# Attention and two MLPs on one core: output stores put off by two steps, a third query buffer, weight stores in tile five, softmax of three batches summed per head by ScalarE

## The chip, the core and the metric

The kernel runs on one core of one Trainium2 chip. TensorE (PE) multiplies, ScalarE (ACT), VectorE (DVE) and GpSimd (POOL) do the elementwise work, and SyncE (SP) issues every DMA of the program, in order, from one queue. Each engine takes its instructions in a fixed order and waits where one is not ready. The metric is the time of one execution on the device in microseconds (us).

## The reference

Three steps follow one another; all data are float32, and the kernel's products keep nearly that precision.

```
# attention, batch 8, heads 8, 576 queries, 64 columns; keys and values are mean-pooled by 8 (72 rows)
scores = q @ k_p.T / sqrt(64); scores -= max(scores); attn = exp(scores)
x = (attn / (sum(attn) + 1e-9)) @ v_p            # -> 4608 tokens x 512
h = x @ w_in1;  x = leaky(h, 0.01) @ w_out1      # 512 -> 2048 -> 512
h = x @ w_in2;  out = relu(h)**2 @ w_out2        # 512 -> 2048 -> 512
```

## The kernel before

**Products.** A float32 product is made of three matmuls (`three`, L271): each operand is split into a high part, cast by ScalarE, and the low rest, subtracted by VectorE. So every operand needs a ScalarE instruction and a VectorE instruction ahead of the matmul.

**First part, up to about 750 us.** The first MLP runs over six tiles of 512 tokens (tile 0 to 5), each as 16 units `f` of 128 hidden columns. `first(t, f)` makes `h` and splits its activation `g` into `gh` and `gl`; `second(t, f)` adds to the four accumulators `acc`. The weights `w` stay decoded in SBUF, and `split_weights` splits them again for each tile into a tile `hl` (a pool of four). In tile 1 those splits are also written to DRAM (`WD`, L190 to L198), from where the later part loads them. Writes that are put off by some ticks pass through `later` and `tick`.

**Work laid between the units.** The generator `attention()` yields after each small step, and the main loop (L900) takes 3 steps per unit in tile 0 and 5 in the later tiles, until the attention is done (in tile 3). A batch has five chunks of 128 or 64 queries: `load_q` fetches a chunk two ahead, `stage_a` transposes it, `stage_b` makes scores `s`, maximum `mx`, exponentials `x`, sums `sm` and the weights `p`, `stage_c` transposes `p`, and `stage_d` makes four output blocks `o` per span, which ScalarE copies to `xo` and SP stores to `x0` in DRAM. `load_x(t + 1)` reads tile t + 1 back from `x0` three units before the tile ends, into `xs`, and `split_x` splits it. `prepare_sums` (`s`, `hs`) and `prepare_products` (`ops`, `hl2`, with its loads `st2`) prepare weight sums for the later part in the same gaps.

**Second part, from about 750 us.** The remaining tokens of the first MLP and then the second MLP run with seven instead of eight block products (`first2`, `second2`), with the weights streamed from `WD`.

**What sets the order.** The program is written in the order above; a list scheduler then orders each engine's instructions by its own estimate, so what stands where on an engine (SP's DMAs too) is read from the built program. In rows of that program `xs1_2_0` is block 0 of the load for tile 2, `xo3_1_0` block 0 of batch 3's second span, `mx1_320_0` the maximum of batch 1's chunk that begins at query 320, `hl_in_4_8` the split of tile 4's unit 8, and the number at a name's end is a counter.

Of the kernel before, what the change touches and what calls it, by code (L numbers as in the profile page):

```python
# [8 lines left out]
F32 = mybir.dt.float32  # L9
# [8 lines left out]
P = 128  # L18
# [9 lines left out]
def raw(ap):  # L28

    return ap.bitcast(F32)  # L30
# [3 lines left out]
def attention_two_mlps(  # L34
# [11 lines left out]
    nc = tc.nc  # L46
    B, H, S, D = q.shape
# [7 lines left out]
    NF = DFF // P  # L55
    RG = KR * H // 2
    SPANS = (320, 256)
    EARLY = 1
    AHEAD = 5
    RATES = (3, 5)  # L60
    HT = 384
    NTILE = 6
# [10 lines left out]
    one_stack = ctx.enter_context(ExitStack())  # L73
    tpool = one_stack.enter_context(tc.tile_pool(name="t", bufs=6))
    hlpool = one_stack.enter_context(tc.tile_pool(name="hl", bufs=4))
    xpool = one_stack.enter_context(tc.tile_pool(name="x", bufs=6))
    gpool = one_stack.enter_context(tc.tile_pool(name="g", bufs=2))
    w_late = one_stack.enter_context(tc.tile_pool(name="w1_late", bufs=NQ))
    w_early_stack = one_stack.enter_context(ExitStack())
# [7 lines left out]
    def temp(name, dt=F32):  # L87
        return tpool.tile([P, TT], dt, tag="t", name=name)

    def work(name, n=TT, early=False):  # L90
        if early:
            return ps_a.tile([P, n], F32, tag="acc", name=name)
        return ps_w.tile([P, n], F32, tag="w", name=name)
# [17 lines left out]
    def place(g):  # L111

        if g < PLAIN:
            return g // TT, g % TT, TT
        return NTILE + (g - PLAIN) // HT, (g - PLAIN) % HT, HT
# [5 lines left out]
    def later(n, **kw):  # L121
        LATE.append([n, kw])

    def tick(n=1):

        for one in LATE:
            one[0] -= n
        while LATE and LATE[0][0] <= 0:
            nc.sync.dma_start(**LATE.pop(0)[1])
# [52 lines left out]
    def split_weights(kind, t, f):  # L182

        w = W[kind, f]
        hl = hlpool.tile([P, 2, TT], F32R, tag="hl", name=f"hl_{kind}_{t}_{f}")
        hi, lo = hl[:, 0], hl[:, 1]
        nc.scalar.copy(hi, w)
        nc.vector.tensor_tensor(out=lo, in0=w, in1=raw(hi), op=ALU.subtract)  # L188
        HL[kind, t, f] = (hi, lo)
        if t == 1:  # L190
            p, i = f % NQ, f // NQ
            for j in range(2):
                part = {(0, 0): 0, (0, 1): 1, (1, 1): 2}.get((i, j) if kind == "in" else (j, i))
                if part is not None:
                    later(
                        2, out=WD[1, kind, p // 2][part, :, p % 2].rearrange("p (h x) -> p h x", h=2),
                        in_=raw(hl)[:, :, j * HD:(j + 1) * HD],
                    )  # L198
# [72 lines left out]
    def three(outp, a, b, first, last, **kw):  # L271

        (ah, al), (bh, bl) = a, b
        nc.tensor.matmul(outp, ah, bh, start=first, stop=False, **kw)  # L274
        nc.tensor.matmul(outp, ah, bl, start=False, stop=False, **kw)  # L275
        nc.tensor.matmul(outp, al, bh, start=False, stop=last, **kw)  # L276


    def attention():

        with ExitStack() as s:
            qp = s.enter_context(tc.tile_pool(name="qp", bufs=2, side="right"))
            ap1 = s.enter_context(tc.tile_pool(name="ap1", bufs=1, side="right"))
            xp = s.enter_context(tc.tile_pool(name="xp", bufs=3, side="right"))
# [151 lines left out]
            for b in range(B):  # L436
                at = 0
                for span in range(len(SPANS)):
                    off = 0
                    while off < SPANS[span]:  # L440
                        n = min(P, SPANS[span] - off)
                        chunks.append((b, span, at, off, n))
                        at, off = at + n, off + n

            qn, qt = {}, {}

            def load_q(b, span, at, off, n):
                qn[b, at] = qp.tile([P, H, D], F32, tag="q", name=f"q{b}_{at}", bufs=2)
                nc.sync.dma_start(out=qn[b, at][:n], in_=q[b, :, at:at + n, :].rearrange("h p d -> p h d"))

            def stage_a(b, span, at, off, n):
# [11 lines left out]
            def stage_b(b, span, at, off, n):  # L463
# [3 lines left out]
                for e in range(2):  # L467
# [10 lines left out]
                    nc.vector.tensor_reduce(out=mx[:n], in_=sc[:n], axis=AX.X, op=ALU.max, negate=True)  # L478
                    if b < EARLY:
                        for h in range(4):  # L480
# [7 lines left out]
                    )  # L488
                if b >= EARLY:
                    nc.scalar.activation(x[:n], x[:n], AF.Exp)  # L490
# [39 lines left out]
            def stage_d(b, span):  # L530
                n = SPANS[span]
                g0 = b * S + sum(SPANS[:span])
                for m in range(NP):
                    o = work(f"o{b}_{span}_{m}")[:, :n]
                    three(
                        o, tuple(t[:, m].rearrange("p a d -> p (a d)") for t in vM),
                        (pt_h[:, m, :n], pt_l[:, m, :n]), True, False,
                    )
                    nc.tensor.matmul(o, vR[:, m], pt_r[:, m // 2, :n], start=False, stop=True)
                    done = 0  # L540
                    if g0 < TT:
                        done = min(n, TT - g0)
                        xh, xl = X[1, 0][m]
                        nc.scalar.copy(xh[:, g0:g0 + done], o[:, :done])
                        nc.vector.tensor_tensor(
                            out=xl[:, g0:g0 + done], in0=o[:, :done], in1=raw(xh[:, g0:g0 + done]), op=ALU.subtract
                        )
                    if done < n:
                        xo = xp.tile([P, SPANS[0]], F32, tag="xo", name=f"xo{b}_{span}_{m}", bufs=2)
                        nc.scalar.copy(xo[:, done:n], o[:, done:n])  # L550
                    while done < n:
                        t, at, wide = place(g0 + done)
                        step = min(n - done, wide - at)
                        nc.sync.dma_start(
                            out=x0[t][m * P:(m + 1) * P, at:at + step], in_=xo[:, done:done + step]
                        )
                        done += step
                    yield

# [10 lines left out]
            for i in range(len(chunks) + 1):  # L570
                if i < len(chunks):
                    b = chunks[i][0]
# [16 lines left out]
                if i > 0:  # L589
                    b, span = chunks[i - 1][:2]  # L590
# [11 lines left out]

    ready = [0]
    att = attention()


    X, XS = {}, {}
# [7 lines left out]
    def load_x(t):  # L615
        XS[t] = []
        for c in range(NK):
            st = temp(f"xs1_{t}_{c}")
            nc.sync.dma_start(out=st, in_=x0[t][c * P:(c + 1) * P, :])
            XS[t].append(st)  # L620

    def split_x(t):
        new_x(t)
        for (hi, lo), st in zip(X[1, t], XS.pop(t)):
            nc.scalar.copy(hi, st)
            nc.vector.tensor_tensor(out=lo, in0=st, in1=raw(hi), op=ALU.subtract)
# [255 lines left out]
        prepare_weights(w1)  # L882
        w1 += 1

    at_work, made, due = True, 0, 0
    prep, preparing, hooks = None, True, 0
    sums1 = prepare_sums()

    def advance():
        nonlocal at_work, made  # L890
        made += 1
        if next(att, 1):
            at_work = False

    split_weights("in", 0, 0)
    split_weights("out", 0, 0)
    first(*units[0])
    split_weights("in", 0, 1)
    x2pool, xg = None, iter(())
    for i, (t, f) in enumerate(units):  # L900
        if f == NF - 3 and t + 1 < NTILE:
            while ready[0] * S < min((t + 2) * TT, NT):
                advance()
            load_x(t + 1)
        if f == NF - 1 and t + 1 < NTILE:
            split_x(t + 1)

        rate = RATES[min(t, 1)]
        if i + 1 < len(units):
            first(*units[i + 1])  # L910
        tick()
        if i + 2 < len(units):
            split_weights("in", *units[i + 2])
        if i + 1 < len(units):
            split_weights("out", *units[i + 1])
        while at_work and made < due + rate // 2:
            advance()
        second(t, f)
        tick()
        due += rate  # L920
        while at_work and made < due:
            advance()
        if w1 < NF:
            prepare_weights(w1)
            w1 += 1
        elif t > 0:
            next(sums1, None)
        if not at_work:
            if prep is None:
                ppool = ctx.enter_context(tc.tile_pool(name="prep", bufs=1, side="right", reuse_waits="tile"))  # L930
                prep = prepare_products()
            for _ in range(3):
                if preparing and next(sums1, 1) and next(prep, 1):
                    preparing = False
        if t == NTILE - 1 and f >= NQ:
            if x2pool is None:
                assert not at_work and next(sums1, 1)
                w_early_stack.close()
                x2pool = ctx.enter_context(tc.tile_pool(name="x2", bufs=1, side="right", reuse_waits="tile"))
                ring = ctx.enter_context(tc.tile_pool(name="ring", bufs=RING, side="right", reuse_waits="tile"))  # L940
                load_x2(0)
                tick(9)
                blocks.insert(0, next_block())
            else:
                if not XO:
                    xg = products_x(0)
                next(xg, None)
# [47 lines left out]
```

## Time and profile before

| | |
|---|---|
| time, median of 3 runs | 1690.49 us (1690.46 to 1691.48) |
| profiled execution: its own time, its span | 1693.28 us, 1691.6 us |
| busy in the span: PE, DVE, ACT, POOL | 1624.4, 1233.9, 840.5, 135.1 us |
| DMA | 403.87 MB, 239 GB/s over the span |

The span goes from the first to the last instruction; 1.7 us of the profiled time lie around it. A busy PE is a PE with a matmul under way, so the difference to the span is time in which it had none. A stage in which PE has no idle time can only be shortened on PE itself.

### The profile page before, as it was taken

The page shows a single profiled execution, that of the slowest core. Times are in us where ns is not written, and L with a number is a line of the kernel's source. Part 1 is how long each engine was busy: PE and PEld are TensorE (multiplying, and loading weights), DVE is VectorE, ACT ScalarE, POOL GpSimd, SP SyncE. Part 2 cuts the span into 40 slices and gives each one's busy share as a digit, 9 for nine tenths or more (in the row PEclk, how much of TensorE's full clock was granted, in tenths as well). Part 3 has the DMA queues.
Part 4 walks back from the last instruction along what each step waited for, and adds up shares of the span by engine and source line. Part 5 has one row for each costly group of instructions (what it writes and reads, how often), then busy time and mean ns, then how long its engine had stood idle before and what let it go on. Part 6 is the DMA issues. An engine that isn't in the chain of part 4 may idle for free.

```text
span 1691.6 us, 26132 instructions
## 1 busy us (share of the span) xinstructions
PE 1624.4 (96%) x9688; PEld 1498.5 (89%) x9688; DVE 1233.9 (73%) x1825; ACT 840.5 (50%) x1377; POOL 135.1 (8%) x149
## 2 busy tenths in 40 slices
PE   4888999799999999999999999999999999999998
PEld 3666787677888888889999999999999999999998
DVE  5899988899867988885736648559378477486484
ACT  5666655555656767765535424325334234244233
POOL 3122223222220000000000000000000000000000
PEclk7799999899999999999999999999999999999999
DMA  7644667775623756878888988988988889888886
GB/s 179 185 156 152 190 212 234 229 228 167 201 60 125 255 197 220 292 255 299 292 288 255 303 275 252 310 263 269 307 252 284 287 256 296 277 249 274 265 254 203
DMA packets 215807, 403.87 MB, mean 239 GB/s; under 512 B 55424, under 2 KB 119936, under 8 KB 215680
## 3 DMA queue, kind: packets, MB, share of 16 engines
q1 hardware_dynamic: 215680, 402.19, 74.0%
q8 instruction: 78, 1.28, 0.3%
q14 instruction: 49, 0.40, 0.1%
HBM read 314.57 MB, written 85.98 MB: 237 GB/s over the span
## 4 chain that ended last, share of the span: by engine, by line
PE 74%; DVE 12%; DMA 6%; ACT 3%; issue 2%; SPq 2%; POOL 0%; DVEq 0%; ACTq 0%; POOLq 0%
PE acc L276 12%; PE acc L275 12%; PE h L274 12%; PE h L276 12%; PE acc L274 12%; PE h L275 12%; DMA st_in_out<-in_moe_w_out_dram 2%; DMA wd_out<-hl_out 1%; DVE gl L644 1%; DVE hl_out L188 1%; PE s L470 1%; SPq L332 1%; DVE hl_in L188 1%; DMA rk<-in_k_dram 1%; DVE v L313 1%
## 5 line engine op out<-in xcount | busy, mean ns | idle before, releaser
L690 ACT CAST oh<-g 128x768 fp32r<-128x768 f32 x224 | 187.2, 836 | 284.2 <-PE acc L275 163.6
L274 PE MATMUL h<-xh,wb_in 128*128 128x384 f32 x896 | 299.4, 334 | 1.0 <-ACT s L779 1.0
L275 PE MATMUL h<-xl,wb_in 128*128 128x384 f32 x896 | 299.3, 334 | 0.0
L276 PE MATMUL h<-xh,wb_in 128*128 128x384 f32 x896 | 299.3, 334 | 0.0
L691 DVE TENSOR_TENSOR ol<-g,oh 128x768 fp32r<-128x768 f32 x224 | 213.6, 955 | 102.1 <-ACT oh L690 101.3
L276 PE MATMUL acc<-wb_out,ol 128*128 128x256 f32 x1008 | 282.2, 280 | 0.0
L274 PE MATMUL acc<-wb_out,oh 128*128 128x256 f32 x1008 | 281.2, 279 | 0.0
L275 PE MATMUL acc<-wb_out,oh 128*128 128x256 f32 x1008 | 281.2, 279 | 0.0
L275 PEld LDWEIGHTS acc<-wb_out,oh 128*128 128x128 f32 x1008 | 189.5, 188 | 0.0
L276 PEld LDWEIGHTS acc<-wb_out,ol 128*128 128x128 f32 x1008 | 189.2, 188 | 0.0
L274 PEld LDWEIGHTS acc<-wb_out,oh 128*128 128x128 f32 x1008 | 188.5, 187 | 0.0
L785 DVE TENSOR_TENSOR g<-h,s 128x768 f32<-128x768 f32 x32 | 30.6, 956 | 196.1 <-PE h L276 120.9
L274 PEld LDWEIGHTS h<-xh,wb_in 128*128 128x128 f32 x896 | 168.2, 188 | 1.3 <-ACT s L779 1.3
L275 PEld LDWEIGHTS h<-xl,wb_in 128*128 128x128 f32 x896 | 168.2, 188 | 0.0
L276 PEld LDWEIGHTS h<-xh,wb_in 128*128 128x128 f32 x896 | 168.2, 188 | 0.0
L274 PE MATMUL acc<-gh,hl_out 128*128 128x512 f32 x384 | 150.9, 403 | 8.8 <-ACT gh L643 8.7
L274 PE MATMUL h<-xh,hl_in 128*128 128x512 f32 x384 | 154.2, 402 | 3.3 <-DVE x L486 2.3
L275 PE MATMUL acc<-gl,hl_out 128*128 128x512 f32 x384 | 151.0, 397 | 6.5 <-DVE gl L644 6.4
L276 PE MATMUL h<-xh,hl_in 128*128 128x512 f32 x384 | 151.6, 395 | 2.2 <-DVE hl_in L188 2.2
L275 PE MATMUL h<-xl,hl_in 128*128 128x512 f32 x384 | 150.9, 393 | 0.0
L276 PE MATMUL acc<-gh,hl_out 128*128 128x512 f32 x384 | 149.2, 394 | 0.4 <-DVE hl_out L188 0.3
L694 DVE TENSOR_TENSOR g<-g,g 128x768 f32<-128x768 f32 x128 | 120.8, 955 | 6.7 <-ACT g L752 5.2
(148 smaller groups left out, 2960.6 us busy)
## 6 DMA issues: line engine op xcount, KB each, us to landing
wb_in<-wd_in SPq DMA_DIRECT2D x224, 512.0 KB, 4.3
wb_out<-wd_out SPq DMA_DIRECT2D x224, 512.0 KB, 4.5
xs<-x SPq DMA_DIRECT2D x16, 768.0 KB, 6.7
out_dram<-o SPq DMA_DIRECT2D x24, 384.0 KB, 5.0
k<-in_k_dram SPq DMA_DIRECT2D x64, 128.0 KB, 3.4
q<-in_q_dram SPq DMA_DIRECT2D x32, 256.0 KB, 4.8
st_in_out<-in_moe_w_in_dram SPq DMA_DIRECT2D x16, 512.0 KB
st_in_out<-in_moe_w_out_dram SPq DMA_DIRECT2D x16, 512.0 KB, 4.7
```

The lines of the kernel that those rows point to most:

```text
L188: nc.vector.tensor_tensor(out=lo, in0=w, in1=raw(hi), op=ALU.subtract)
L274: nc.tensor.matmul(outp, ah, bh, start=first, stop=False, **kw)
L275: nc.tensor.matmul(outp, ah, bl, start=False, stop=False, **kw)
L276: nc.tensor.matmul(outp, al, bh, start=False, stop=last, **kw)
L313: nc.vector.tensor_tensor(out=dst if n == D else src[:, :, 0:n], in0=src[:, :, 0:n], in1=src[:, :, n:2 * n], op=ALU.add)
L332: nc.sync.dma_start(out=ts[-1][a * KM:(a + 1) * KM, m % 2], in_=src[b, heads[m][a], 0:KM * POOL, :].rearrange("(kk j) d -> kk (j d)", j=POOL),
L470: nc.tensor.matmul(sc[:n, 2 * m:2 * m + 2].rearrange("p a x -> p (a x)"), qT[:, 2 * e + m, :n], kT[b % 2][:, 2 * e + m].rearrange("p a x - ...
L644: nc.vector.tensor_tensor(out=gl, in0=g, in1=raw(gh), op=ALU.subtract)
L690: nc.scalar.copy(hi, src)
L691: nc.vector.tensor_tensor(out=lo, in0=src, in1=raw(hi), op=ALU.subtract)
L694: nc.vector.tensor_tensor(out=out_, in0=a, in1=b, op=ALU.subtract)
L785: nc.vector.tensor_tensor(out=g11, in0=v, in1=s1, op=ALU.add)
```

## The change

It has five parts. (1) The softmax form that batch 0 alone used (`EARLY`) is used for batches 0 to 2: ScalarE makes the exponentials per head, straight from the scores, with the maximum as bias, and sums them in the same instruction; in the other form VectorE subtracts the maximum and sums. (2) The stores of `xo` go into a list, and are issued when two further attention steps have been made, or just ahead of `load_x`; `xo` has three buffers instead of two. (3) The query tile has three buffers instead of two. (4) The splits of the plain weights are written to DRAM in tile 4 (the fifth) instead of tile 1. (5) The pool of split activations has 5 buffers per tag instead of 6.

```
-    EARLY = 1
+    EARLY = 3
...
-    xpool = one_stack.enter_context(tc.tile_pool(name="x", bufs=6))
+    xpool = one_stack.enter_context(tc.tile_pool(name="x", bufs=5))
...
-        if t == 1:
+        if t == NTILE - 2:
...
-                qn[b, at] = qp.tile([P, H, D], F32, tag="q", name=f"q{b}_{at}", bufs=2)
+                qn[b, at] = qp.tile([P, H, D], F32, tag="q", name=f"q{b}_{at}", bufs=3)
...
-                        xo = xp.tile([P, SPANS[0]], F32, tag="xo", name=f"xo{b}_{span}_{m}", bufs=2)
+                        xo = xp.tile([P, SPANS[0]], F32, tag="xo", name=f"xo{b}_{span}_{m}", bufs=3)
                         nc.scalar.copy(xo[:, done:n], o[:, done:n])
                     while done < n:
                         t, at, wide = place(g0 + done)
                         step = min(n - done, wide - at)
-                        nc.sync.dma_start(
+                        STORES.append((made, dict(
                             out=x0[t][m * P:(m + 1) * P, at:at + step], in_=xo[:, done:done + step]
-                        )
+                        )))
...
+    STORES, made = [], 0
+
+    def put_stores(until):
+
+        while STORES and STORES[0][0] <= until:
+            nc.sync.dma_start(**STORES.pop(0)[1])
...
+    put_stores(made)
...
         made += 1
         if next(att, 1):
             at_work = False
+        put_stores(made - 2 if at_work else made)
...
             while ready[0] * S < min((t + 2) * TT, NT):
                 advance()
+            put_stores(made)
             load_x(t + 1)
```

**SP's queue ahead of the loads for tile 2.** Before:

```order
L554 DMA x0_4_101<-xo3_1_3_3081 128x256
L129 DMA wd1_out2_125<-hl_out_1_12_3045 128x2x256 x2
L412 DMA rx4_3154<-rv4_3152 32x256 x6
L129 DMA wd1_out1_124<-hs1_out2_3116 128x4x512
L341 DMA rk5_3180<-in_k_dram 64x1x512
L332 DMA k5_0_3182<-in_k_dram 64x512 x4
L332 DMA k5_2_3187<-in_k_dram 64x512 x4
L619 DMA xs1_2_0_3215<-x0_2_99 128x512
```

The same place now:

```order
L449 DMA q4_448_3248<-in_q_dram 128x8x64
L129 DMA wd1_in2_121<-hs1_in4_3720 128x4x512
L341 DMA rk6_3861<-in_k_dram 64x1x512
L610 DMA x0_4_101<-xo3_1_0_3018 128x256
L129 DMA wd1_out2_125<-hs1_out4_3912 128x4x512
L610 DMA x0_4_101<-xo3_1_1_3055 128x256
L610 DMA x0_4_101<-xo3_1_2_3062 128x256
L610 DMA x0_4_101<-xo3_1_3_3082 128x256
L449 DMA q5_0_3304<-in_q_dram 128x8x64
L412 DMA rx5_3818<-rv5_3816 32x256 x2
L625 DMA xs1_2_0_3215<-x0_2_99 128x512
```

Behind the last store of batch 3 stood 18 transfers before the first load `xs1_2_0`; now three stand there. The key loads of batch 5 have moved ahead of all four stores, and the weight sums' writes (`hs1`) are by pairs 4 instead of pair 2, so VectorE's work for them stands earlier too.

**VectorE at the softmax of batch 1's chunk 320, in tile 0.** Before:

```order
L478 TENSOR_REDUCE mx1_320_0_1144<-s1_320_0_1141 128x4
L162 SCALAR_TENSOR_TENSOR wm_1_9_1085<-st1_in9_out9_1081,wm_1_9_1085 128x1024
L486 TENSOR_TENSOR x1_320_1138<-s1_320_0_1141,mx1_320_0_1144 128x288
L172 ISA w1_9_1084<-wm_1_9_1085,w1_9_1084 128x2048
L478 TENSOR_REDUCE mx1_320_1_1150<-s1_320_1_1147 128x4
L515 TENSOR_TENSOR pt_l_172<-pt1_256_1161,pt_h_171 128x4x64
L486 TENSOR_TENSOR x1_320_1138<-s1_320_1_1147,mx1_320_1_1150 128x288
L155 TENSOR_SCALAR wm_1_10_1172<-wm_1_10_1172 128x1024
L644 TENSOR_TENSOR gl1_0_7_1195<-g1_0_7_1192,gh1_0_7_1194 128x512
L491 TENSOR_REDUCE sm1_320_1139<-x1_320_1138 128x8
```

ScalarE there now, where one exponential of 128x576 stood:

```order
L153 ACTIVATE wm_1_9_1097<-st1_in9_out9_1093 128x1024
L187 CAST hl_in_0_8_1214<-w1_8_1009 128x512
L481 ACTIVATE x1_320_1150,sm1_320_1151<-s1_320_0_1153,mx1_320_0_1156 128x72 x4
L481 ACTIVATE x1_320_1150,sm1_320_1151<-s1_320_1_1162,mx1_320_1_1165 128x72 x4
L171 ACTIVATE w1_10_1187<-st1_in10_out10_1184 128x1024
L646 ACTIVATE g1_0_7_1208<-h1_0_7_1195 128x512
```

The two L486 and the L491 leave VectorE (the two L478 stay), and eight exponentials with sums stand on ScalarE in one piece, ahead of the activation `g` of unit 7.

**SP's queue in tile 4.** Before:

```order
L129 DMA wd2_in1_128<-hl2_in2_3_6241 128x4x512
L145 DMA st2_out3_out11_6518<-in_moe2_w_out_dram 128x1024 x2
L129 DMA wd2_out1_132<-hl2_out2_0_6374 128x3x512
L129 DMA wd2_out1_132<-hl2_out2_3_6379 128x4x512
L140 DMA st2_in4_in12_6656<-in_moe2_w_in_dram 128x4x256 x2
L129 DMA wd2_in1_128<-hl2_in3_0_6510 128x3x512
L129 DMA wd2_in1_128<-hl2_in3_3_6515 128x4x512
```

The later part of the same stretch now:

```order
L129 DMA wd2_out1_132<-hl2_out2_3_6391 128x4x512
L129 DMA wd1_in0_119<-hl_in_4_8_6416 128x2x256
L129 DMA wd1_out3_126<-hl_out_4_7_6419 128x2x256
L140 DMA st2_in4_in12_6685<-in_moe2_w_in_dram 128x4x256 x2
L129 DMA wd1_in0_119<-hl_in_4_9_6465 128x2x256
L129 DMA wd1_out0_123<-hl_out_4_8_6468 128x2x256 x2
L129 DMA wd2_in1_128<-hl2_in3_0_6530 128x3x512
L129 DMA wd1_in1_120<-hl_in_4_10_6512 128x2x256
L129 DMA wd1_out0_123<-hl_out_4_9_6515 128x2x256 x2
L129 DMA wd2_in1_128<-hl2_in3_3_6535 128x4x512
```

Three writes of 128x2x256 per unit stand between the loads and writes of the prepared products, 48 in all, and the prepared products themselves come a little later: between the loads for tile 4 and the end of that tile stand ten loads `st2` where there were fourteen, and twelve writes `hl2` where there were fourteen.

## Rows read from the trace of the kernel before

**Rows 1.** The page, part 1: busy us (share of the span) xinstructions.

```profile
PE 1624.4 (96%) x9688; PEld 1498.5 (89%) x9688; DVE 1233.9 (73%) x1825; ACT 840.5 (50%) x1377; POOL 135.1 (8%) x149
```

**Rows 2.** Windows, cut near the tiles: tiles 0, 1, 2, 4, and the second part.

```profile
core 0: us, PE busy (x) PEld busy (x) DVE busy (x) ACT busy (x) POOL busy (x), PEclk, DMA share, GB/s
60.00:184.00 124.00, 113.40 (x524) 88.34 (x522) 116.34 (x195) 79.44 (x142) 26.93 (x24) 0.96 0.53 163
184.00:322.00 138.00, 124.89 (x649) 102.24 (x650) 122.72 (x251) 77.26 (x153) 40.82 (x38) 0.97 0.74 227
322.00:460.00 138.00, 133.43 (x700) 109.22 (x700) 120.45 (x246) 80.32 (x165) 33.76 (x38) 0.99 0.66 202
...
571.00:660.00 89.00, 89.00 (x395) 73.68 (x394) 78.29 (x129) 64.52 (x108) 0.00 (x0) 1.00 0.65 227
...
846.00:1691.00 845.00, 840.99 (x5822) 840.79 (x5820) 530.20 (x583) 321.26 (x397) 0.00 (x0) 1.00 0.84 271
```

**Rows 3.** Waits of PE in tile 0: us in total, times, longest.

```profile
PE pt L513 <- POOL p L495: 2.5, 2, 1.9
PE h L276 <- DVE hl_in L188: 2.2, 2, 1.5
```

**Rows 4.** Timeline of SP at tile 1's end: start, us, what was issued.

```profile
282.33 1.03 SPq L129 DMA_DIRECT2D wd_in<-hs_in  x1
291.86 0.33 SPq L554 DMA_DIRECT2D x<-xo  x1
...
305.18 6.17 SPq L332 DMA_DIRECT2D k<-in_k_dram  x8
311.39 2.01 SPq L619 DMA_DIRECT2D xs<-x  x4
```

**Rows 5.** Timeline of ACT and PE there: in brackets the idle time before.

```profile
315.87 0.62 ACT L625 CAST xh<-xs 128x512 fp32r<-128x512 f32 x1 [4.34 <-DMA xs<-x]
...
317.06 0.80 PE L274 MATMUL acc<-gh,hl_out 128*128 128x512 f32 x1 [6.70 <-ACT gh L643]
...
319.89 0.80 PE L275 MATMUL acc<-gl,hl_out 128*128 128x512 f32 x1 [2.04 <-DVE gl L644]
```

**Rows 6.** Windows of 4 us around that wait.

```profile
312.00:316.00 4.00, 0.00 (x0) 0.00 (x0) 3.94 (x11) 0.13 (x1) 1.68 (x2) 0.69 0.99 229
316.00:320.00 4.00, 0.90 (x2) 0.40 (x2) 3.93 (x11) 2.18 (x5) 0.00 (x0) 0.50 1.10 363
```

**Rows 7.** Groups by form on DVE: xcount | busy us, mean ns | idle before.

```profile
L486 DVE TENSOR_TENSOR x<-s,mx 128x288 f32<-128x288 f32 x56 | 23.7, 448 | 0.1
L491 DVE TENSOR_REDUCE sm<-x 128x8 f32<-128x576 f32 x28 | 20.9, 748 | 2.2 <-ACT x L490 2.1
L220 DVE TENSOR_TENSOR hs_out<-s_out,hs_out 128x1024 fp32r<-128x1024 f32 x8 | 9.9, 1235 | 3.2 <-ACT hs_out L219 3.2
L203 DVE TENSOR_TENSOR s_out<-w,w 128x256 f32<-128x256 f32 x8 | 4.3, 543 | 0.1
```

**Rows 8.** Group of the exponential on ACT, then batch 0's form in the timeline.

```profile
L490 ACT ACTIVATE x<-x 128x576 f32<-128x576 f32 x28 | 19.2, 687 | 25.2 <-DVE x L486 25.0
...
15.89 0.31 ACT L481 ACTIVATE x<-s,mx 128x72 f32<-128x72 f32 x1
...
16.19 0.32 ACT L481 ACTIVATE x<-s,mx 128x72 f32<-128x72 f32 x1
```

**Rows 9.** DMA issues: xcount, KB each, median us to landing.

```profile
wd_in<-hl_in SPq DMA_DIRECT2D x24, 256.0 KB, 3.0
wd_out<-hl_out SPq DMA_DIRECT2D x24, 256.0 KB, 3.6
```

**Rows 10.** Window of 10 us with the most DMA traffic between 500 and 790 us.

```profile
700.00:710.00 10.00, 10.00 (x46) 8.28 (x45) 9.85 (x18) 9.66 (x16) 0.00 (x0) 1.00 1.03 372
```

**Rows 11.** Waits of ACT and SP over the span.

```profile
ACT hl_in L187 <- DMA wd_in<-hl_in: 3.5, 3, 1.3
...
SPq L129 <- DVE hl_in L261: 79.6, 16, 8.6
```

More of the change, by code (lines that the diff above doesn't have):

```diff
@@ L883, in attention_two_mlps @@
         w1 += 1
-    at_work, made, due = True, 0, 0
+    put_stores(made)
+    at_work, due = True, 0
     prep, preparing, hooks = None, True, 0
```

## Prediction

> **What bounds the kernel now.** I began with the page's busy times: PE works in 96% of the span and VectorE in 73% [rows 1], so 67 us in all are open on PE, and the question is where they lie. The windows by stage answer that. In the second part PE idles 4 of 845 us, and in tile 4 none of 89 [rows 2]: nothing is to be won there but by less matmul work, which this change does not bring. PE idles 10.6 us in tile 0 (124 less 113.40), 13.1 us in tile 1 (138 less 124.89) and 4.6 us in tile 2. The granted clock, 0.96, 0.97 and 0.99 there, adds: a share of 0.04, 0.03 and 0.01 of PE's busy time, 4.5, 3.7 and 1.3 us. So at most 15.1, 16.8 and 5.9 us are open in the three tiles, 37.8 us together. The first 60 us have waits too, but the loads and copies that end them stand in the same order as before, so I count nothing there.
>
> What ends PE's waits differs. In tile 0 VectorE is busy in 116.34 of 124 us, 94%, and PE waits mostly for splits and for softmax weights that come from VectorE's results [rows 2, 3]. In tile 1 one event is most of it. SP sat behind a store of `xo` until 291.86, having issued the transfer before it at 282.33; the keys of batch 5 then went out from 305.18 on, and only behind them, at 311.39, the four loads of tile 2's tokens [rows 4]. ScalarE, in order, waited 4.34 us for the first of these with the cast `gh` behind it, so PE waited 6.70 us for `gh` and 2.04 us for `gl` [rows 5], 8.7 us together. The clock came down to 0.69 and 0.50 in that wait [rows 6]; 0.50 is the lower of the two levels, 1.2 GHz.
>
> **The change, part by part.**
>
> Softmax on ScalarE. Of each chunk in batches 1 and 2, VectorE loses two subtractions of 0.448 us and one sum of 0.748 us [rows 7], 1.64 us. Seven of these ten chunks lie in tile 0 (batch 1's five and two of batch 2 in PE's order), 11.5 us, and three in tile 1, 4.9 us. ScalarE gains eight exponentials and loses one. In batch 0 they start 0.30 us apart (15.89 to 16.19), so a chunk takes 2.4 us instead of 0.687 [rows 8], 1.7 us more, 12 us in tile 0. That engine was busy 79.44 of 124 us there, and goes to 74%. The cover is that slack. Without it all ten chunks would lie on the path, 17 us, because `g` and `gh` are queued behind the eight. I take 1 us, near the lower end, as a chunk's 2.4 us is about half of what one unit's matmuls take (tile 4: 89 us for 16 units, 5.6 us). The Trainium skill, page "ScalarE: Activation LUTs", section "Rules for kernel authors", budgets about 0.3 us per ACTIVATE plus 0.83 ns per element. By that rule, as an estimate, eight of 72 columns cost 2.9 us; the trace shows 2.4 us.
>
> What is freed is not all given to PE. VectorE's order shows that the scheduler pulls other work forward: by the loads of tile 2 the weight sums stand three further on, each some four operations of about 0.54 us and one of 1.235 us [rows 7], 3.4 us. So tile 1 gets 10 us of VectorE work and loses 4.9 us. Its 122.72 us become about 128, which is a floor for tile 1, 10 us under its 138. At the 94% that tile 0 reached it would be 136 us. This filling work then is gone from tile 2.
>
> Stores put off, third buffers. SP no longer stands behind `xo` with the key loads in the queue: tile 2's loads follow the last store of batch 3 with three transfers between instead of 18. The first of that batch's stores went out at 291.86 in the old trace and the others followed block by block, so the loads can go out between then and 311.39; I take the middle, 10 us earlier, which is ahead of their use. The price is that a buffer's store is issued two steps later; three buffers instead of two give the same distance to reuse. I cost it at nothing; if it fails, ScalarE waits for landings, as in the bound of the last rival.
>
> So of PE's idle time I take back about half in each tile: 5 us in tile 0, 6.5 in tile 1, 3 in tile 2. The lower bound is nothing (other work fills the gap, the clock falls elsewhere), the upper the 37.8 us above.
>
> Weight stores in tile 4. 48 stores of 256 KB, 12.6 MB, leave tile 1, where landing took 3.0 and 3.6 us [rows 9], and come to tile 4. There DMA moved 227 GB/s for 89 us, 20.2 MB, at a share of 0.65. With all of it, 32.8 MB would pass in 89 us, 368 GB/s; the densest stretch of 10 us in this part had 372 GB/s [rows 10]. The new order moves four loads and two stores of prepared products, 3.9 MB, out of the tile, so 28.9 MB remain. At tile 4's own bytes per share (227 / 0.65 = 349 GB/s) they need 83 us and fit. At tile 1's (227 / 0.74 = 307 GB/s) they need 94 us, 5 more than there are. For 32.8 MB that rate gives 107 us, 18 more. PE has no idle time in tile 4, so what is lost there is lost in full. A split reuses the buffer of the one two units before. Its store has about 11 us to be issued and land, and the cast that waits for it stands between `g` and `gh`. In tile 1 such waits were 3.5 us in all, but SP also stood up to 8.6 us behind writes of prepared products [rows 11], and now these stores queue behind those. I take 3 us, between 0 and 18.
>
> On the other side stands a figure of the Trainium skill. Its page "DMA: Bandwidth & Descriptors", section "Specifications", gives about 358 GB/s as the HBM limit per core. By that rule, as an estimate, 32.8 MB would take 92 us, 3 over the tile. The trace's 372 GB/s lies above it, so I do not treat it as a wall.
>
> Five buffers instead of six. One fewer block of the next tile can be split before the last unit's matmuls let go of the old ones. The scheduler moved three of the four casts behind them. The last unit's accumulation hides this; without it some 0.6 us per cast at five tile changes, 3 us. I take 0.
>
> Sum: -5 - 6.5 - 3 + 3 + 1 = -10.5 us. The profiled execution takes 1693.28 us, so 1682.8; it lies 2.8 us above the median of the runs, 1690.49, and from that I forecast **1680 us**.
>
> **Rivals.**
> 1. All of it comes back. PE becomes the only bound in tiles 0 to 2, and tile 4 holds. For it: the largest wait has one cause, which the order removes. Against it: VectorE is at 94% and gets filling work. Some 25 of the 37.8 us: 1665.
> 2. Nothing moves: the work pulled forward, or eight exponentials ahead of `gh`, takes the place of what was freed, and tile 4 costs what the rest brings. For it: tile 1's floor of 128 us at 94% is 136. About 1690.
> 3. Slower, by tile 4. If nothing moved out of it helps and transfers go at tile 1's 307 GB/s, it is DMA that sets its length, +18 instead of +3: -14.5 + 1 + 18 = +4.5, 1695. It decides once tile 4 loses more than 13.5 us, that is below 320 GB/s for 32.8 MB. Against it: the order spreads the stores and thins the rest.
> 4. Slower, by ScalarE. The 17 us lie on the path of `gh`, or casts wait for late stores as long: -14.5 + 3 + 17 = +5.5, 1696. Against it: 74% busy.
>
> **How the numbers follow.** Chances: forecast 0.48, rival 1 0.17, rival 2 0.15, rival 3 0.13, rival 4 0.07. A measurement of this kernel tells about 0.2%, 3.4 us, from no change. Faster by more: 0.65, from the first two; within it: 0.15; slower: 0.20. The range goes from 1664, which leaves the best outcomes of rival 1 out, to 1696, beyond which a tenth remains. The forecast's own range is 1673 to 1686.
>
> **What would show it.** VectorE should have 30 instructions fewer and ScalarE 70 exponentials more, at 0.30 us each. The four loads of tile 2 should go out before ScalarE wants them, with no wait of PE above 2 us and no drop of the clock at the change from tile 1 to 2. PE's idle time in tiles 0 to 2 should fall from 28.3 to about 14 us. Tile 4's DMA share should be about 0.9, with waits of ScalarE's `hl` casts for `wd`, and PE should idle no more than a few us. I am wrong if tile 4 grows by over 10 us, if PE waits for exponentials or `gh` behind them, or if VectorE's filling work keeps tile 1 at its 138 us.

## The result, and the profile after

The changed kernel takes 1666.43 us (median of 4 runs, 1665.64 to 1667.88) beside 1690.99 us for the kernel before (4 runs, 1690.46 to 1691.65): a ratio of 0.9853, 95% interval 0.9838 to 0.9868, 24.6 us less. The profiled execution took 1667.88 us, its span 1666.1 us. The forecast was 1680: the direction was right, and the gain came out more than twice as large as the 10.5 us of the prediction's sum.

Busy time over the span, page of the changed kernel, as in [rows 1]:

```profile
PE 1615.4 (97%) x9688; PEld 1496.2 (90%) x9688; DVE 1219.9 (73%) x1795; ACT 858.3 (52%) x1527; POOL 132.5 (8%) x149
```

VectorE has 30 instructions fewer. The span is 25.5 us shorter: PE's idle time fell from 67.2 to 50.7 us, and its busy time by 9.0 us with the same 9688 matmuls. The cuts of [rows 2] don't move with the tiles, so here every tile ends where VectorE starts its last copy of `acc`. First the kernel before, tiles 0 to 5 (columns as in [rows 2]):

```profile
60.00:193.70 133.70, 122.77 (x571) 95.95 (x570) 125.94 (x214) 86.56 (x154) 28.65 (x25) 0.96 0.54 165
193.70:339.30 145.60, 132.59 (x689) 108.86 (x688) 125.46 (x257) 80.95 (x165) 42.87 (x41) 0.96 0.73 225
339.30:472.30 133.00, 127.47 (x673) 104.05 (x672) 120.22 (x246) 77.98 (x158) 33.84 (x39) 1.00 0.62 189
472.30:574.20 101.90, 101.90 (x500) 84.94 (x499) 75.45 (x136) 65.76 (x122) 9.04 (x15) 1.00 0.40 135
574.20:661.50 87.30, 87.30 (x387) 72.29 (x386) 76.62 (x124) 62.83 (x105) 0.00 (x0) 1.00 0.64 223
661.50:747.20 85.70, 84.64 (x374) 69.77 (x373) 75.44 (x118) 57.91 (x95) 0.00 (x0) 1.00 0.71 246
```

The same windows of the changed kernel:

```profile
60.00:186.10 126.10, 121.78 (x586) 98.17 (x586) 121.23 (x206) 100.82 (x262) 29.20 (x25) 0.97 0.64 191
186.10:319.70 133.60, 127.12 (x672) 104.40 (x672) 127.97 (x264) 86.53 (x207) 41.39 (x41) 1.00 0.63 196
319.70:447.00 127.30, 125.08 (x671) 104.04 (x670) 107.76 (x217) 74.83 (x156) 32.62 (x40) 1.00 0.47 137
447.00:551.00 104.00, 103.94 (x510) 86.67 (x509) 83.45 (x148) 70.97 (x129) 8.99 (x14) 1.00 0.50 169
551.00:636.60 85.60, 85.60 (x380) 70.87 (x379) 66.36 (x105) 56.29 (x93) 0.00 (x0) 1.00 0.92 315
636.60:723.20 86.60, 85.23 (x375) 70.04 (x374) 78.62 (x125) 60.45 (x99) 0.00 (x0) 1.00 0.74 253
```

Tile 0 is 7.6 us shorter, tile 1 12.0, tile 2 5.7; tiles 3 to 5 together are 1.3 longer. In tiles 0 to 2 PE's idle time (length less busy) fell from 10.9, 13.0 and 5.5 to 4.3, 6.5 and 2.2 us. Tile 1's clock went from 0.96 to 1.00. Tile 4 moves 315 instead of 223 GB/s, and PE has no gap in it.

At the end of tile 1, SP's timeline answers [rows 4]:

```profile
283.98 3.31 SPq L610 DMA_DIRECT2D x<-xo  x3
287.38 0.40 SPq L449 DMA_DIRECT2D q<-in_q_dram  x1
289.46 1.22 SPq L412 DMA_DIRECT2D rx<-rv  x2
290.74 2.00 SPq L625 DMA_DIRECT2D xs<-x  x4
```

The loads of tile 2 go out at 290.74 instead of 311.39, ScalarE does not wait for them, and the waits of 6.70 and 2.04 us of [rows 5] are gone. The longest waits of PE from 60 to 345 us, in the columns of [rows 3], were these in the kernel before:

```profile
PE acc L274 <- ACT gh L643: 8.4, 5, 6.7
PE acc L275 <- DVE gl L644: 5.3, 4, 2.0
```

They are small now:

```profile
PE h L274 <- DVE x L486: 2.2, 3, 1.1
PE pt L513 <- POOL p L495: 2.2, 3, 1.2
PE pr L522 <- DVE pt_l L515: 2.0, 2, 1.3
```

### The profile page after: what moved, and what is told of

Its sections match the earlier page's. It is cut to its first block, busy times and chain, and to the rows that moved or that the text cites. A ratio compares the mean times of both kernels' runs of the same rounds, so it can differ in the third digit from the quotient of the medians.

```text
span 1666.1 us, 26276 instructions
## 1 busy us (share of the span) xinstructions
PE 1615.4 (97%) x9688; PEld 1496.2 (90%) x9688; DVE 1219.9 (73%) x1795; ACT 858.3 (52%) x1527; POOL 132.5 (8%) x149
## 4 chain that ended last, share of the span: by engine, by line
PE 77%; DVE 14%; ACT 3%; DMA 3%; issue 2%; SPq 1%; POOL 0%; DVEq 0%; ACTq 0%; POOLq 0%
PE acc L276 12%; PE h L274 12%; PE acc L275 12%; PE acc L274 12%; PE h L275 12%; PE h L276 12%; DVE gl L650 1%; DVE hl_out L188 1%; PE s L470 1%; DVE hl_in L188 1%; DVE v L313 1%; DMA st_in_out<-in_moe_w_out_dram 1%; DVE mx L478 1%; ACT x L481 1%; DMA xs<-x 1%
## 5 line engine op out<-in xcount | busy, mean ns | idle before, releaser
L274 PE MATMUL acc<-gh,hl_out 128*128 128x512 f32 x384 | 153.7, 402 | 0.7 <-ACT gh L649 0.7
L276 PE MATMUL acc<-gh,hl_out 128*128 128x512 f32 x384 | 150.9, 393 | 1.1 <-DVE hl_out L188 1.1
```

## The experiments

Three theories stood against each other. **1**: two causes add; the softmax form frees VectorE in tile 0, and taking the 48 weight stores out of tile 1 clears SP's queue at its end. **2**: VectorE's time alone. **3**: the one late load at the end of tile 1, with the clock that falls in it. Each kernel was timed beside the kernel before on the same chip (1691.0 to 1692.3 us there).

| kernel | us | ratio to before, 95% interval |
|---|---|---|
| softmax form, batches 0 to 2, alone | 1670.02 | 0.9872 (0.9857 to 0.9888) |
| softmax form, batches 0 and 1, alone | 1678.76 | 0.9927 (0.9914 to 0.9939) |
| weight stores in tile 4 alone | 1684.85 | 0.9958 (0.9946 to 0.9971) |
| `xo` stores late and third `xo`, x pool 5 | 1692.27 | 1.0005 (0.9996 to 1.0013) |
| third query buffer, x pool 5 | 1682.57 | 0.9945 (0.9933 to 0.9958) |
| x pool 5 alone | 1691.76 | 1.0002 (0.9991 to 1.0014) |
| softmax form, third query buffer, x pool 5 | 1663.68 | 0.9839 (0.9825 to 0.9852) |
| softmax form, VectorE's old work kept | 1695.34 | 1.0023 (1.0014 to 1.0032) |
| changed, old softmax form | 1686.22 | 0.9968 (0.9955 to 0.9980) |
| changed, `xo` stores at once | 1667.32 | 0.9858 (0.9843 to 0.9873) |
| changed, two query buffers | 1668.20 | 0.9864 (0.9851 to 0.9878) |
| changed, weight stores in tile 1 | 1664.12 | 0.9838 (0.9825 to 0.9852) |
| the same, softmax form to batch 4 | 1661.88 | 0.9830 (0.9817 to 0.9843) |
| the same, softmax form to batch 7 | 1664.57 | 0.9845 (0.9832 to 0.9859) |
| changed, weight stores of tile 4 twice | 1687.31 | 0.9970 (0.9962 to 0.9979) |

### Softmax form alone

```
-    EARLY = 1
+    EARLY = 3
```

Expected: 

> The kernel before with the softmax form of batches 0 to 2 alone. Theory 1 (two causes that add: softmax frees VectorE in tile 0, and the queue of SP at the end of tile 1 is cleared by taking the 48 weight stores out of that tile): tile 0 is some 8 us shorter, as in the changed kernel (VectorE's last copy of acc there at about 186 instead of 193.7), tile 1 keeps most of its late loads, because in SP's order four key loads and 12 other transfers still stand between the first store of batch 3 and the loads for tile 2; 1680 to 1683 us. Theory 2 (it is VectorE alone, 16.4 us freed): about 1672. Theory 3 (it is only the one late load at the end of tile 1, with the clock that falls in it): 1690, no change.

It took 1670.0 us: 22 of the 24.6 us. Its windows of tiles 0 and 1, and SP's timeline:

```profile
60.00:185.20 125.20, 120.59 (x585) 96.68 (x584) 121.31 (x206) 101.01 (x262) 29.53 (x25) 0.98 0.65 197
185.20:315.90 130.70, 127.86 (x675) 105.08 (x674) 116.38 (x234) 83.11 (x206) 34.99 (x41) 1.00 0.74 232
```

```profile
277.62 2.21 SPq L554 DMA_DIRECT2D x<-xo  x2
...
284.88 5.01 SPq L332 DMA_DIRECT2D k<-in_k_dram  x8
289.94 2.01 SPq L619 DMA_DIRECT2D xs<-x  x4
```

```profile
293.96 0.62 ACT L625 CAST xh<-xs 128x512 fp32r<-128x512 f32 x1
```

Tile 0 is 8.5 us shorter and tile 1 14.9 us, although the eight key loads still stand ahead of the loads for tile 2. But nothing is late: SP no longer stands 9.5 us behind the first `xo`, and the loads go out at 289.94, 4.0 us before ScalarE casts them (293.96) without a wait. Theory 3 falls here as the whole cause, as tile 0 ends long before that load. Theory 1 falls in one part: SP's queue need not be cleared for that load to be in time.

### The other parts alone

The stores in tile 4:

```
-        if t == 1:
+        if t == NTILE - 2:
```

Expected: 

> The kernel before with the weight stores in tile 4 alone. Theory 1: in SP's order the key loads of batch 5 are gone from between the stores of batch 3 and the loads for tile 2, so the wait of 8.7 us of PE at the change from tile 1 to 2 goes, and the lower clock behind it; tile 4 pays nothing, as in the changed kernel (PE idle 0 there): 11 to 16 us faster, 1675 to 1680. Theory 2 (VectorE alone): no change, 1690. The prediction as it stands: tile 4 pays 3 us and the queue stays blocked by the stores of xo, since only putting them off frees it: 1693.

The late `xo` stores, with the list and the calls of `put_stores` as in the diff of the change:

```
-    xpool = one_stack.enter_context(tc.tile_pool(name="x", bufs=6))
+    xpool = one_stack.enter_context(tc.tile_pool(name="x", bufs=5))
...
-                        xo = xp.tile([P, SPANS[0]], F32, tag="xo", name=f"xo{b}_{span}_{m}", bufs=2)
+                        xo = xp.tile([P, SPANS[0]], F32, tag="xo", name=f"xo{b}_{span}_{m}", bufs=3)
...
-                        nc.sync.dma_start(
+                        STORES.append((made, dict(
```

Expected: 

> The kernel before with the stores of xo put off and its third buffer, and the x pool at 5 (the third buffer of xo needs that room). The prediction as it stands: this is what frees SP at the end of tile 1, 6.5 us of PE's idle time there: 1684. Theory 1: SP's order shows the 18 transfers ahead of the loads for tile 2 nearly as before (the stores of batch 3 a few places nearer, the key loads of batch 5 still behind them), so the late load stays: 1688 to 1692, no change.

The third query buffer, with the same line of the x pool:

```
-                qn[b, at] = qp.tile([P, H, D], F32, tag="q", name=f"q{b}_{at}", bufs=2)
+                qn[b, at] = qp.tile([P, H, D], F32, tag="q", name=f"q{b}_{at}", bufs=3)
```

Expected: 

> The kernel before with a third query buffer and the x pool at 5, nothing else. All theories: no change, within 2 us of 1691. If the x pool's smaller size costs what the prediction gave as its bound, 0.6 us per cast at five tile changes, it is up to 3 us slower.

That line of the x pool by itself. Expected: 

> The kernel before with the x pool at 5, nothing else. The kernel with this and a third query buffer was 9 us faster. If the query buffer is the cause: 1690 to 1693 here. If the smaller pool is (its casts stand later on ScalarE's order at each tile change, ahead of nothing that PE wants): 1682 to 1685.

The late stores gave nothing, so what the prediction held to free SP does not: the key loads still stand ahead, the loads for tile 2 go out at 307.37 instead of 311.39, and ScalarE waits for them nearly as long as in [rows 5].

```profile
307.37 2.01 SPq L625 DMA_DIRECT2D xs<-x  x4
```

```profile
311.77 0.62 ACT L631 CAST xh<-xs 128x512 fp32r<-128x512 f32 x1 [3.97 <-DMA xs<-x]
```

The weight stores gave 7 us, less than theory 1 and more than theory 2 had. With them gone from tile 1 the loads go out early (299.69, ScalarE waits 0.55 us for them), but VectorE is then busy in 134.29 of tile 1's 140.60 us, and PE waits for it instead:

```profile
191.80:332.40 140.60, 130.67 (x685) 107.61 (x684) 134.29 (x275) 81.41 (x163) 41.22 (x41) 0.99 0.60 184
```

The buffers gave 9 us, which no theory had; the pool alone gave nothing, so it is the query buffer. It shows in the waits of SP, over the whole span, that end with a chunk's transpose, in the kernel before:

```profile
SPq L449 <- PE trq L455: 31.9, 11, 6.3
```

and with the third buffer:

```profile
SPq L449 <- PE trq L455: 16.0, 7, 5.7
```

### Parts taken out of the changed kernel

The edits above, each the other way round. `EARLY = 1`. Expected: 

> The changed kernel with batches 1 and 2 back in VectorE's form of the softmax. Theory 1 (softmax and the cleared queue add): tile 0 takes its 8 us back and tile 1 a few, because VectorE was busy in 96% of it after the change: 1675 to 1679. Theory 2 (VectorE alone): 1688. Theory 3 (only the one late load): 1667, as the changed kernel.

`nc.sync.dma_start(` for `STORES.append(`. Expected: 

> The changed kernel with each store of xo issued at once (three buffers kept). Theory 1: SP's order ahead of the loads for tile 2 stays the same list, so no change: 1665 to 1669. The prediction as it stands: the put-off frees the queue, so 6.5 us are lost: 1673.

`if t == 1:`. Expected: 

> The changed kernel with the weight stores back in tile 1. Theory 1: SP's queue is full again at the end of tile 1 and the loads for tile 2 come late: 11 to 16 us slower, 1678 to 1683. The prediction as it stands (the stores in tile 4 cost 3 us there, the put-off frees SP): 1664. Theory 2 (VectorE alone): 1667.

`bufs=2` for the query tile. Expected: 

> The changed kernel with two query buffers. If the third query buffer is what made the kernel with the third buffer and the smaller x pool 9 us faster than before, and if that adds to the rest: 1670 to 1676. If its gain was in the same waits that the softmax form takes away: 1665 to 1669.

Without the softmax form 20 us are lost, where theory 3 had none. In that kernel the loads of tile 2 are early, and the longest waits of PE from 60 to 345 us name VectorE's subtraction `x`, and the weights `p` that POOL makes behind it:

```profile
299.04 3.69 SPq L625 DMA_DIRECT2D xs<-x  x4
```

```profile
PE h L274 <- DVE x L486: 7.0, 5, 3.2
PE pt L513 <- POOL p L495: 5.8, 4, 2.1
```

So the other four parts together, with the late load mended, win some 5 us (ratio 0.9968), and the rest hangs on the softmax form. Each of the other three, taken out alone, changes nothing that can be told apart: with the weight stores back in tile 1 the kernel is 2.3 us faster by the medians, but the intervals overlap.

### VectorE's time or the shorter chain

The softmax form also takes two steps out of the chain from scores to weights. Here, in the kernel before with `EARLY = 3` and the x pool at 5, VectorE makes these two steps all the same, into `xj` and `sj`, which nobody reads:

```
+                        if b > 0:
+                            nc.vector.tensor_tensor(
+                                out=xj[:n, hs], in0=sc[:n], in1=mx[:n].to_broadcast([n, 4, SP]), op=ALU.add
+                            )
...
+                if 0 < b < EARLY:
+                    nc.vector.tensor_reduce(out=sj[:n], in_=xj[:n], axis=AX.X, op=ALU.add)
```

Expected: 

> The kernel with the softmax form of batches 0 to 2 alone (1670.0 us), where VectorE still makes the subtractions and sums of batches 1 and 2, into tiles that nobody reads (the x pool is at 5 for their room). The output stays the reference's. It tells VectorE's time from the shorter chain of softmax (maximum to weights with two steps fewer). Theory 2a, VectorE's time is what counts: its 16.4 us are back, and so is the time, 1686 to 1692. Theory 2b, the chain counts (the subtractions and sums no longer stand between the scores and the weights): it stays at 1668 to 1674.

All of the gain is gone, and 4 us more: theory 2a of that expectation. Tiles 0 and 1 take 136.9 and 144.1 us:

```profile
60.00:196.90 136.90, 125.44 (x585) 99.37 (x585) 126.56 (x218) 99.48 (x261) 27.40 (x25) 0.95 0.54 163
196.90:341.00 144.10, 129.78 (x673) 106.15 (x673) 124.84 (x253) 84.81 (x207) 36.30 (x41) 0.96 0.73 225
```

With VectorE's work the late load is back too. ScalarE's and PE's timelines and the clock there read nearly as in [rows 5, 6]:

```profile
316.67 0.62 ACT L634 CAST xh<-xs 128x512 fp32r<-128x512 f32 x1 [2.76 <-DMA xs<-x]
```

```profile
317.86 0.79 PE L274 MATMUL acc<-gh,hl_out 128*128 128x512 f32 x1 [5.89 <-ACT gh L652]
321.30 0.79 PE L275 MATMUL acc<-gl,hl_out 128*128 128x512 f32 x1 [2.65 <-DVE gl L653]
```

```profile
316.00:320.00 4.00, 0.79 (x1) 0.28 (x1) 3.90 (x13) 1.63 (x3) 1.38 (x2) 0.50 1.07 374
```

One thing differs from the kernel before: VectorE reads the scores beside ScalarE, so it also holds their buffer, and PE waits for that once, 0.9 us. The 4.3 us above the kernel before I put down to this and to ScalarE's 70 further exponentials; no run parts the two.

The form for batches 0 and 1 alone (`EARLY = 2` in the kernel before). Expected: 

> The kernel before with the softmax form for batches 0 and 1 alone, whose five chunks lie in tile 0: VectorE loses 8.2 us there. If VectorE's time sets the time in both tiles, tile 0 is some 6 us shorter and tile 1 as it was: 1683 to 1686. If the late loads of tile 2 hang on batch 2's softmax in tile 1, they stay late here: 8.7 us of PE's waiting stays. If they go as well (PE's largest wait under 2 us), about 1675.

It gave 12 us, between the cases: tile 0 ends at 185.0 instead of 193.7, and tile 1 takes 139.4 instead of 145.6 us. ScalarE no longer waits for the load, and PE's waits for `gh` from 60 to 345 us come to 3.5 us in all, where one alone was 6.70 [rows 5]; one of 2.8 us for `gl` stays. At that place ScalarE now waits 3.36 us for VectorE's subtraction, with `gh` behind it.

### How near tile 4 is to the limit of transfers

```
-                    later(
-                        2, out=WD[1, kind, p // 2][part, :, p % 2].rearrange("p (h x) -> p h x", h=2),
...
+                    for dst in (WD[1, kind, p // 2], WX[kind, p // 2]):
+                        later(
+                            2, out=dst[part, :, p % 2].rearrange("p (h x) -> p h x", h=2),
```

Expected: 

> The changed kernel with each weight store of tile 4 issued a second time, to DRAM that nobody reads: 12.6 MB more in the 89 us that moved 28.0 MB. If tile 4 is near the limit of transfers, the 40.6 MB need 109 us at the 371 GB/s of its densest 10 us: 20 us more, or less if part of them slides into tile 5, whose share is 0.74. If there is slack in buffers of hl and of the queue, PE stays without a gap in tile 4 and the time is within 3 us of 1666.

It took 20.9 us more by the medians. Window of its tile 4, then the longest waits of ScalarE and PE there that name a split of weights:

```profile
549.00:652.80 103.80, 94.35 (x383) 73.22 (x382) 61.42 (x97) 53.19 (x87) 0.00 (x0) 0.95 0.95 324
```

```profile
ACT hl_out L192 <- DMA wx_out<-hl_out: 12.5, 6, 3.0
...
PE h L280 <- ACT hl_in L192: 6.2, 4, 2.8
```

The tile grew by 18.2 us, the case of the prediction's rival 3: a cast waits until the store of the buffer's last use has landed, and PE waits for the cast. The changed kernel moves 27.0 MB in this tile (315 GB/s in 85.6 us), this one 33.6 MB, at a lower clock as well (0.95). At 324 GB/s tile 4 has room for 27.7 MB in its 85.6 us, so by this estimate the changed kernel lies just below the edge. Not every one of the 12.6 MB more was paid for: tile 5 moved 286 instead of 253 GB/s and took 86.5 us, as before the doubling (86.6).

### What is left

`EARLY = 3`, the query tile's `bufs=3` and the x pool's `bufs=5` in the kernel before. Expected: 

> The kernel before with the softmax form of batches 0 to 2, the x pool at 5 and the third query buffer. With the stores put off besides it took 1664.1. If the put-off is worth nothing: 1662 to 1666. If the buffers' 9 us and the softmax's 22 add in full: 1661. If the buffers' gain is in waits that the softmax form takes away, as with the weight stores in tile 4: 1668 to 1671.

The changed kernel with `if t == 1:` and `EARLY = 5`. Expected: 

> The changed kernel with the weight stores back in tile 1 (1664.1 us) and the softmax form for batches 0 to 4. Batches 3 and 4 lie mostly in tiles 1 and 2, where VectorE was busy in 115 of 130 and 119 of 132 us and PE idles 2.4 and 4.1 us: if VectorE's time still counts there, 3 to 5 us faster, 1659 to 1661; if PE's work is all that is left, 1662 to 1664; if 80 more exponentials hold up the activations behind them on ScalarE, slower than 1665.

The same with `EARLY = 8`. Expected: 

> As the version with the form for batches 0 to 4 (1661.9 us), now for all eight batches. Tile 2 has 3 to 4 us of PE's idle time and batches 5 to 7 lie in tiles 2 and 3, where VectorE is busy in 90% and 75%: at most 3 us faster, 1659; if PE is all that is left, 1661 to 1664; ScalarE is busy about 60% in tiles 2 and 3 and should not hold anything up.

The three edits of the first of these kernels are enough for 1663.7 us: late stores and moved weight stores add nothing. The form for five batches has the lowest median here, 1661.9 us, but its interval, 0.9817 to 0.9843, overlaps those of the changed kernel and of the two at 1664 us. Its tile 1:

```profile
186.00:314.20 128.20, 125.65 (x670) 103.98 (x669) 100.77 (x209) 97.62 (x337) 34.37 (x40) 1.00 0.76 234
```

VectorE went from 115.4 us, in the kernel with three batches, to 100.8 us there, and the tile got 1.7 us shorter: with 2.6 us of idle time PE is the bound now. The form for all batches gives nothing more.

## Why the prediction was right in direction and wrong in size

**What was right.** The places (tiles 0 to 2), VectorE's 30 instructions, and ScalarE's exponentials 0.30 us apart:

```profile
114.46 0.32 ACT L481 ACTIVATE x<-s,mx 128x72 f32<-128x72 f32 x1
...
114.77 0.31 ACT L481 ACTIVATE x<-s,mx 128x72 f32<-128x72 f32 x1
```

PE's idle time in tiles 0 to 2 was to fall to about 14 us and is 13.0. Tile 1's work on VectorE was foreseen as about 128 us and is 127.97, but that is partly luck: the weight sums (L203 to L220) grew by 5.9 us there, not by 10, and the preparation of keys and values (L313) by 6.1 us, which the prediction did not have.

**The step that failed** is the sum, "-5 - 6.5 - 3 + 3 + 1 = -10.5 us", in what it leaves out and in its two costs. Its terms of idle time, from "So of PE's idle time I take back about half in each tile", were 5, 6.5 and 3 us and measured 6.6, 6.5 and 3.3, 16.4 against 14.5: near enough. But the prediction had itself counted 9.5 us of lower clock as open, and without a reason it gave none of that back: PE's busy time stands in the sum as nothing, and it fell by 7.9 us. From 60 us to the end of tile 5 PE's idle time fell by 16.1 us (30.5 to 14.4) and its busy time by 7.9 (656.7 to 648.8). In windows of 10 us from 60 us on, one less the granted clock, times PE's busy time, sums to 7.2 us before and 3.5 after: 3.7 of the 7.9 are clock. The other 4.2 us of busy time I have not traced. The remaining 1.5 us of the span lie behind tile 5.

**The terms of the other sign.** "I take 3 us" for the weight stores in tile 4: tiles 4 and 5 together take 173.0 us before and 172.2 after, so 0. The estimate of 28.9 MB for the tile was close (27.0), and it fitted, as the better of the two rates said. The bound of 18 us more at 32.8 MB was of the right size: with the stores doubled, 33.6 MB took 18.2 us more. "I take 1 us" for ScalarE: no wait of PE above 0.3 us names an exponential in the changed kernel, so I see no loss there; where VectorE's work was kept, it was at most 4.3 us. So the sum should have read -16.4 - 7.9 and nothing on the other side. That is the time of rival 1 ("All of it comes back", 1665), but not its condition: PE is not the only bound in tiles 0 to 2, where it still idles 13.0 us and VectorE is busy in 96% of tiles 0 and 1.

**A cause that was put in the wrong place.** A second step failed that the sum hides: under "Stores put off, third buffers" the late load was laid on SP's queue, and its mending on the late stores. The runs show one cause for most of tile 0's and tile 1's loss, VectorE's time: the late stores alone leave the load late (1692.3 us), the softmax form alone takes the late load away with the key loads still in the queue, and VectorE's old work brings it back. So that tile 1's term of 6.5 us came out to the tenth is luck. VectorE's share of 94% in tile 0 was carried over to tile 1 as its ceiling (136 us for 128 us of work). In the changed kernel it reaches 96% in both (121.23 of 126.10, 127.97 of 133.60), and 99% in a window of 10 us in which PE runs without a gap:

```profile
230.00:240.00 10.00, 10.00 (x54) 8.46 (x53) 9.91 (x18) 4.88 (x10) 3.25 (x2) 1.00 0.59 182
```

The prediction had VectorE's freed time filled by work that the scheduler pulls forward. With the softmax form alone it is not filled: tile 1 has 116.38 us of VectorE's work, and 8 of the weight sums' subtractions (L220), as in the kernel before. With the weight stores moved alone it has 10, with both 12. So it is the move of the weight stores that pulls the weight sums forward, and it costs tile 1 what it gives tile 2: with the stores back in tile 1 the two tiles take 129.9 and 131.8 us, in the changed kernel 133.6 and 127.3.

The Trainium skill, page "Perfetto Trace Analysis", section "Optimizing Scalar/DVE Operations", says that work may be moved to ScalarE if VectorE is saturated. These runs agree: 16.4 us of VectorE's work gave 22 us while it was full, and the work of two further batches at most some 2 us, not clear of the noise, once PE was the bound.

**Rivals 2 to 4** did not occur. Nothing took the place of the wait removed, tile 4 has no gap on PE, and ScalarE, busy in 101 of tile 0's 126 us (80%, where the prediction had 74%), held PE up by nothing that shows.

**What stays open.** The query buffer gives 9 us alone, 6 beside the softmax form, and 2 or nothing in the changed kernel. The gain lies in small pieces over tiles 0 to 5 and I have no single wait for it. The parts' gains alone (22, 9 and 7 us) are over the 24.6 of the whole, so they work in part on the same slack. A scheduler orders every one of these kernels anew, so a difference of 2 us in one tile of one profile means little.

## What to carry to other kernels

Where an engine is nearly full in a stage, as VectorE was here at 94% of tile 0, suspect it as the bound even where the waits name a queue or a late load: give it less work there first, and see which of the other waits are left. When a wait goes, count the clock that fell in it too, and add it to the idle time. Before moving traffic into a stage where PE has no gap, divide the bytes of that stage by its length: here 27.0 MB in 85.6 us (315 GB/s) passed unseen, and 33.6 MB took 103.8 us (324 GB/s).

## What had not been expected of the hardware

With the stores doubled, DMA held 324 GB/s over 104 us at a share of 0.95, while single windows of 10 us show more, in the changed kernel:

```profile
620.00:630.00 10.00, 10.00 (x46) 8.27 (x45) 9.57 (x18) 8.00 (x15) 0.00 (x0) 1.00 1.05 371
```

So the peak of a short window, which the prediction set beside the need of a whole tile, is some 15% above what DMA held over that tile. An exponential with its sum is followed by a read of the sum (0.19 to 0.24 us) and still starts every 0.30 us: the read lies beside the next exponential.
